# Moving stores and read-back loads from SyncE's DMA queue to GpSimd's in a fused attention and feed-forward kernel

## The chip, the cores and the metric

The kernel runs on one core of a Trainium2 chip. The metric is the device time of one execution in microseconds; shown is the median over the runs.

## The reference

```python
def _attn_ref(q, k, v, cap):                      # q, k, v: (4, 12, 448, 64) float32
    scale = 1.0 / np.sqrt(q.shape[-1])
    scores = scale * np.matmul(q, k.transpose(0, 1, 3, 2))
    scores = cap * np.tanh(scores / cap)          # cap = 30
    scores = scores - np.max(scores, axis=-1, keepdims=True)
    attn = np.exp(scores)
    attn = attn / (np.sum(attn, axis=-1, keepdims=True) + 1e-09)
    return np.matmul(attn, v).astype(np.float32)

def _moe_ref(x, w_in, w_out):                     # (1792, 768), (768, 2048), (2048, 768)
    h = x @ w_in
    g = h - np.tanh(h)
    return (g @ w_out).astype(np.float32)
```

x is the attention output with the heads of a token side by side. The two weights arrive as float64, everything else as float32.

## The kernel before

**Two streams of work.** Attention goes through 4 batches of 6 pairs of heads. Its scores are matmuls at `L735` (`fs`, from `fqst`, `fkst`, `fql`, `fkz`), emptied by ScalarE at `L743`; the exponentials are ScalarE's at `L828`, the values and row sums TensorE's at `L963` to `L987` and `L1054` to `L1062`, with sums over blocks of `fe` made by VectorE first (`fes`, `L922`, `L1029`, `L1037`). For some pairs the tails are folded: VectorE transposes and reduces (`fnum`, `fpart`, `L1089`, `L1092`) and TensorE multiplies `fpart` by a constant (`L1101`).

The feed-forward part goes through 64 steps of one slice of 128 hidden units each, for one batch at a time: `fh` = x times a slice of `w_in` (`L1425` to `L1427`, 18 matmuls of 128x384), ScalarE's tanh into `fg` (`L1438`), VectorE's `fg` = h - tanh h (`L1440`), a split of `fg` into a high part `fgh` and a low part `fgl`, and products with a slice of `w_out` that collect in the banks `facc` (`L1478`). The steps run as the segments (batch 0, slices 0 to 9), (1, 0 to 15), (0, 10 to 15), (2, all 16), (3, all 16). At the end of the first segment the sums of batch 0 are put into DRAM (`fyk`, `keep_y`, `L1641`) and read back when its other slices are due. Steps of the feed-forward part and pairs of the attention of later batches are interleaved.

**Weights.** A slice is used by up to four batches. The first time, its raw float64 words (`fw`) are loaded by SyncE's queue and decoded by VectorE in three passes (`L1278`, `L1285`, `L1292`) into `fu`, a tile of 128x1536 float32 (768 KB, the slice of `w_in` and that of `w_out` side by side). GpSimd's queue stores `fu` to DRAM as `fuk` (`L1220`, 16 stores). At the other 48 steps, 10 to 19 and 26 to 63, `fetch_w` loads it back (`fu<-fuk`, `L1209`) through SyncE's queue. There are two slots for `fu`. From `fu` each half is split: a cast to the high part `fwi` or `fwo` (`L475` where ScalarE does it, `L477` where VectorE does) and a subtraction for the low part on VectorE (`L486`). The same split makes `fkst`, `fqst`, `fgh` and `fxh`.

**Output.** A batch's sums are evicted to tiles `fo` and stored by `put` (`L1697`), through SyncE's queue except for one half of the very last one.

**What sets the order.** A planner in the kernel's own code (`Plan.schedule`) lays all instructions on five queues (TensorE, ScalarE, VectorE, SyncE, GpSimd) by a table of costs, with due times, the buffers' slots and the time at which each transfer lands, and the program is emitted in that order. An instruction that both ScalarE and VectorE can do (kind "AD", the casts) goes to VectorE only where ScalarE would be later by more than a bias; before 80 us of planned time the bias is the second number of a setting, later 500 ns. `run` plans with three settings (bias 0, 200, 500) and keeps the plan that ends first. A DMA's issue is priced in `dma`, 620 ns on SyncE and 600 elsewhere, and each queue may have seven transfers on the way:

```python
SETTINGS = [(0.0, 0.0), (0.0, 200.0), (0.0, 500.0)]
c = ISSUE + 60.0 * long if eng == "SP" else 600.0
```

Of the kernel before, what the change touches and what calls it, by code (L numbers as in the profile page):

```python
# [54 lines left out]

AHEAD = 3

BIAS, SWITCH = 500.0, 80000.0

EARLY_W = (10000.0, 40000.0)  # L60
# [20 lines left out]
LANES = 7  # L81

ISSUE, RAW_OUT = 620.0, "SP"
SLOW = dict(qk=2.3, v=2.1, w_in=2.0, w_out=0.95, kept=1.3, keep=0.75)


# [16 lines left out]
class Op:  # L103
    __slots__ = (
        "eng", "cost", "fn", "deps", "alloc", "later", "uses", "key", "due", "n", "succ", "need", "ready", "dma",
        "weight", "end", "lag", "glue",
    )


class Plan:  # L110
# [19 lines left out]
    def op(self, eng, cost, fn, deps=(), alloc=(), uses=(), key=1e18, dma=0.0, weight=1.0, lag=0.0):  # L130
        o = Op()
        o.eng, o.cost, o.fn, o.due, o.dma, o.weight, o.lag = eng, cost, fn, key, dma, weight, lag
        o.deps = [d for d in deps if d is not None]
        o.alloc, o.later = list(alloc), list(uses)
        o.uses = o.alloc + o.later
        o.glue = None
        o.n, o.succ = len(self.ops), []
        for d in o.deps:
            d.succ.append(o)
        for b in o.uses:  # L140
            b.users += 1
        self.ops.append(o)
        return o
# [6 lines left out]
    def schedule(self, wait, bias):  # L150
# [3 lines left out]
        for o in reversed(self.ops):  # L154
            o.key = o.due
            c = min(o.cost) if o.eng == "AD" else o.cost
            if o.dma:
                c += DMA_START + o.dma + DMA_END
            for s in o.succ:
                o.key = min(o.key, s.key - c - self.latency(o, s))  # L160
            o.need, o.ready, o.end = len(o.deps), 0.0, None
        for b in self.bufs:
            b.live, b.left, b.free_at, b.last, b.held = False, b.users, 0.0, None, 0.0
        engines = ["PE", "A", "D", "SP", "PL"]
        free = dict(zip(engines, START))
# [46 lines left out]
        def commit(t, e, o):  # L212

            nonlocal dma_free
            for b in o.alloc:
                s = slots[b.tag]
                b.slot = taken[b.tag] % len(s)
                s[b.slot] = None
                taken[b.tag] += 1
                b.live = True  # L220
            if e == "PE":
                free[e] = t + clock.run(t, o.cost, o.weight, True)
            else:
                free[e] = t + cost(o, e, t)
            o.end = free[e]
            if o.dma:
                begin = max(free[e] + DMA_START, dma_free)
                dma_free = begin + o.dma
                o.end = dma_free + DMA_END
                sent[e].append(o.end)  # L230
            order.append((o, e))
            if o in pools[e]:
                pools[e].remove(o)
            if o.eng == "AD":
                pools["D" if e == "A" else "A"].remove(o)
            for s in o.succ:
                s.ready = max(s.ready, o.end + o.lag + self.latency(o, s))
                s.need -= 1
                if not s.need:
                    put(s)  # L240
            for b in o.uses:
                b.left -= 1
                if b.bank and e != "PE":
                    b.last, b.held = e, o.end
                b.free_at = max(b.free_at, o.end + LAT)
                if not b.left:
                    slots[b.tag][b.slot] = b.free_at
            return 1

        for o in self.ops:  # L250
            if not o.need:
                put(o)
        left = len(self.ops)
        while left:
            cands = {}
            for e in engines:
                found = []
                for o in pools[e]:
                    t = start(o, e)
# [22 lines left out]
            t, e, o = best  # L282
            done = commit(t, e, o)
            while o.glue:
                o = o.glue
# [5 lines left out]
    def patient(self, e, cands, free, cost, wait):  # L291
# [17 lines left out]
                return c  # L309
        return None  # L310

    def run(self, settings, near=None, then=None, after=None):
        best = min((self.schedule(*s) for s in settings), key=lambda r: r[0])
        last = max(n for n, (o, e) in enumerate(best[1]) if e == "PE" or o is after)
        for n, (o, e) in enumerate(best[1]):
            if near and o.end > best[0] - NEAR:
                near()
                near = None
            for b in o.alloc:
                b.tile = self.make(b)  # L320
            if o.eng == "AD":
                o.fn(e)
            else:
                o.fn()
            if then and n == last:
                then()
# [33 lines left out]
class Build:  # L360
# [120 lines left out]
    def split(self, n, hi, lo, x, deps, allocs=((), ()), uses=((), ()), key=1e18, half=False):  # L481

        o1 = self.copy(n, hi, x, deps, allocs[0], uses[0], key=key, half=half)
        o2 = self.dve(
            n,
            lambda: self.nc.vector.tensor_sub(lo(), x(), hi().bitcast(F32)),  # L486
            [o1] + list(deps),
            allocs[1],
            uses[1],
            key=key,  # L490
        )
        return o1, o2

    def dma(self, eng, nbytes, fn, deps=(), alloc=(), uses=(), slow=1, long=False, key=1e18, lag=0.0):
        c = ISSUE + 60.0 * long if eng == "SP" else 600.0
# [44 lines left out]
    def fetch_qk(self, b, p, np_):  # L540
# [4 lines left out]
        for nm, src in (("q", self.q), ("k", self.k)):  # L545
            raw = self.plan.buf(nm + "raw", [128, 2, S // 32, 32])
            ops = []
            for i in range(4):
# [5 lines left out]
                def fn(i=i, h=h, dh=dh, raw=raw, src=src, queue=nc.scalar if eng == "A" else nc.sync):  # L554
# [6 lines left out]
                    self.dma(  # L561
                        eng, np_ * S * 128, fn, [], [] if ops else [raw], [raw] if ops else [], slow=SLOW["qk"],
                        lag=QK_LAG if (b, p) > (0, 1) else 0.0, key=-1e6 + 1e5 * p if also else 1e18,
# [5 lines left out]
    def fetch_v(self, b, p):  # L569
# [3 lines left out]
        for hp in range(2):  # L573
# [3 lines left out]
            for part in range(2):  # L577
# [4 lines left out]
                def fn(hp=hp, at=at, part=part, full=full, tail=tail, queue=nc.gpsimd if also else nc.sync):  # L582
# [3 lines left out]
                    else:  # L586
# [4 lines left out]
                        eng, (TAIL if part else FULL) * 256, fn, [], [] if ops else [vr],  # L591
                        [vr] if ops else [], slow=SLOW["v"], long=True, lag=V_LAG if (b, p) > (0, 0) else 0.0,
                        key=-5e5 + 1e5 * p if also else 1e18,
# [609 lines left out]
    def fetch_w(self, i, f):  # L1203

        nc, DM, plan = self.nc, self.DM, self.plan
        if f in self.kept_op:
            u = plan.buf("u", [128, 2, DM])
            o = self.dma(
                "SP", 8 * 128 * DM, lambda: nc.sync.dma_start(out=u(), in_=self.u_kept[f]), [self.kept_op[f]], [u],  # L1209
                slow=SLOW["kept"], lag=KEPT_LAG,  # L1210
            )
            return u, [o]
        raw, ops = self.fetch_raw(
            f, self.cast_ops[i - AHEAD][:1] if f >= self.segments[0][2] else [],
            key=EARLY_W[f] if f < len(EARLY_W) and not self.general else 1e18, lag=RAW_LAG,
        )
        u = plan.buf("u", [128, 2, DM])
        us = [self.decode(u, raw, ops)]
        o = self.dma(
            "PL", 8 * 128 * DM, lambda: nc.gpsimd.dma_start(out=self.u_kept[f], in_=u()), us, [], [u],  # L1220
            slow=SLOW["keep"], key=self.at + 40000,
        )
        self.kept_op[f] = o
        return u, us

    def fetch_raw(self, f, deps=(), key=1e18, lag=0.0):
# [4 lines left out]
        for hp in range(2):  # L1231

            def fn(hp=hp):
# [6 lines left out]
                self.dma(  # L1240
                    "SP", 4 * 128 * DM, fn, deps, [] if ops else [raw], [raw] if ops else [], slow=SLOW["w_in"], long=True, key=key,
                    lag=lag,
# [5 lines left out]
                RAW_OUT, 8 * 128 * DM, lambda: queue.dma_start(out=raw()[:, 1, :], in_=self.w_out[cols, :]),  # L1248
                deps, [], [raw], slow=SLOW["w_out"], key=key, lag=lag,
            )  # L1250
# [383 lines left out]
    def keep_y(self, m):  # L1634

        nc, k, self.y_ops[m] = self.nc, self.at + 3000, []
        for i in (0, 1, 2):
            o, ops = self.evict(i, self.plan.buf("o", [128, self.DM]), (), k)
            self.y_ops[m].append(
                self.dma(  # L1640
                    "SP", 512 * self.DM, lambda i=i, o=o: nc.sync.dma_start(out=self.y_kept[m][i], in_=o()), ops, [], [o],  # L1641
                    key=self.at + 20000,
                )
            )
        self.acc, self.acc_op = {}, {}
# [40 lines left out]
    def put(self, i, m, o, deps, cols):  # L1686
        nc, S, T = self.nc, self.S, self.TAIL
        if i < 3:
            r = S * m + 128 * i
            parts = [(slice(0, 128), self.out[r : r + 128, cols])]  # L1690
        else:

            tails = self.out.rearrange("(b s) c -> b s c", s=S)[2 * (i - 3) : 2 * (i - 3) + 2, self.FULL :, cols]
            parts = [(slice(T * j, T * j + T), tails[j]) for j in range(2)]
        for rows, out in parts:

            def fn(rows=rows, out=out, q=nc.scalar if cols.start else nc.sync):  # L1697
                q.dma_start(out=out, in_=o()[rows, cols])

            self.dma(  # L1700
                "A" if cols.start else "SP", (rows.stop - rows.start) * (cols.stop - cols.start) * 4, fn, deps, [],
                [o], key=self.at + 20000,
            )

# [129 lines left out]
```

## Time and profile before

| | us |
|---|---|
| median of 3 runs (lowest, highest) | 664.56 (664.21, 664.62) |
| the profiled execution, its whole time | 664.87 |
| its span in the trace | 663.1 |
| TensorE matmuls busy | 649.7 (98%) |
| VectorE busy | 505.3 (76%) |
| ScalarE busy | 444.5 (67%) |
| GpSimd busy | 24.9 (4%) |

The span runs from the first to the last instruction in the trace; the whole time has 1.8 us around it. The granted TensorE clock was 0.999 of full speed over the span. The chain of work that ended last is 85% TensorE, 6% VectorE, 4% ScalarE and 3% DMA. Issues of DMAs do not count as busy on SyncE.

### The profile page before, as it was taken

The page shows a single profiled execution, that of the slowest core. Times are in us where ns is not written, and L with a number is a line of the kernel's source. Part 1 is how long each engine was busy: PE and PEld are TensorE (multiplying, and loading weights), DVE is VectorE, ACT ScalarE, POOL GpSimd, SP SyncE. Part 2 cuts the span into 40 slices and gives each one's busy share as a digit, 9 for nine tenths or more (in the row PEclk, how much of TensorE's full clock was granted, in tenths as well). Part 3 has the DMA queues.
Part 4 walks back from the last instruction along what each step waited for, and adds up shares of the span by engine and source line. Part 5 has one row for each costly group of instructions (what it writes and reads, how often), then busy time and mean ns, then how long its engine had stood idle before and what let it go on. Part 6 is the DMA issues. An engine that isn't in the chain of part 4 may idle for free.

```text
span 663.1 us, 10078 instructions
## 1 busy us (share of the span) xinstructions
PE 649.7 (98%) x3690; PEld 535.6 (81%) x3690; DVE 505.3 (76%) x805; ACT 444.5 (67%) x760; POOL 24.9 (4%) x56
## 2 busy tenths in 40 slices
PE   8999999999999999999999999999999999999996
PEld 5333777786989898898797996987999999999996
DVE  5899999999997989999989599597573343433432
ACT  5999798875775474777874796795375545555444
POOL 5021000000000000000000000000000000000000
PEclk9999999999999999999999999999999999999999
DMA  9999999999793969768963967657776754456513
GB/s 136 201 208 229 307 202 266 242 236 237 234 211 122 245 205 259 229 217 268 255 190 111 276 191 211 199 144 210 235 265 188 191 142 139 133 158 191 148 43 124
DMA packets 156503, 132.59 MB, mean 200 GB/s; under 512 B 112544, under 2 KB 140896, under 8 KB 156448
## 3 DMA queue, kind: packets, MB, share of 16 engines
q1 hardware_dynamic: 149152, 115.89, 68.4%
q0 software_dynamic: 3424, 15.40, 6.6%
q10 hardware_dynamic: 3872, 0.59, 0.7%
q8 instruction: 31, 0.51, 0.3%
q14 instruction: 24, 0.20, 0.1%
HBM read 110.23 MB, written 21.63 MB: 199 GB/s over the span
## 4 chain that ended last, share of the span: by engine, by line
PE 85%; DVE 6%; ACT 4%; DMA 3%; issue 1%; SPq 0%; ACTq 0%; DVEq 0%
PE facc L1478 28%; PE fh L1425 11%; PE fh L1427 11%; PE fh L1426 11%; PE fs L735 6%; PE fs L972 5%; PE fs L1478 3%; PE fs L963 3%; PE fs L1054 2%; PE facc L764 2%; ACT fe L828 2%; DMA fw<-in_moe_w_out_dram 1%; ACT fe L743 1%; DMA fkraw<-in_k_dram 1%; PE fs L978 1%
## 5 line engine op out<-in xcount | busy, mean ns | idle before, releaser
L1478 PE MATMUL facc<-fwo,fgh 128*128 128x512 f32 (+1 forms) x768 | 166.2, 338 | 0.0
L1478 PEld LDWEIGHTS facc<-fwo,fgh 128*128 128x128 f32 x768 | 121.5, 188 | 17.3 <-issue 2.8
L1425 PE MATMUL fh<-fxh,fwi 128*128 128x384 f32 x384 | 131.6, 343 | 0.5 <-DVE fg L1440 0.5
L1427 PE MATMUL fh<-fxh,fwi 128*128 128x384 f32 x384 | 129.9, 338 | 0.0
L1426 PE MATMUL fh<-fxl,fwi 128*128 128x384 f32 x384 | 128.5, 335 | 0.0
L1478 PE MATMUL facc<-fwo,fgl 128*128 128x512 f32 (+1 forms) x384 | 98.8, 338 | 0.0
L828 ACT ACTIVATE fe<-fe,absc 128x896 f32<-128x896 f32 (+1 forms) x96 | 89.3, 962 | 1.3
L1440 DVE TENSOR_TENSOR fg<-fh,fg 128x384 f32<-128x384 f32 x64 | 35.4, 553 | 70.5 <-ACT fg L1438 70.3
L1425 PEld LDWEIGHTS fh<-fxh,fwi 128*128 128x128 f32 x384 | 72.1, 188 | 10.8 <-issue 4.9
L486 DVE TENSOR_TENSOR fwi<-fu,fwi 128x768 fp32r<-128x768 f32 x66 | 62.8, 952 | 19.5 <-ACT fwi L475 19.2
L1438 ACT ACTIVATE fg<-fh 128x384 f32<-128x384 f32 x64 | 31.2, 488 | 66.5 <-PE fh L1427 66.4
L1426 PEld LDWEIGHTS fh<-fxl,fwi 128*128 128x128 f32 x384 | 72.2, 188 | 0.5
L1427 PEld LDWEIGHTS fh<-fxh,fwi 128*128 128x128 f32 x384 | 72.0, 187 | 0.1
L475 ACT CAST fwi<-fu 128x768 fp32r<-128x768 f32 x53 | 44.2, 834 | 39.4 <-PE fh L1427 29.1
L743 ACT ACTIVATE fe<-fs 128x448 f32<-128x448 f32 x112 | 55.6, 542 | 15.7 <-PE fs L735 15.6
L486 DVE TENSOR_TENSOR fwo<-fu,fwo 128x768 fp32r<-128x768 f32 x66 | 62.6, 949 | 4.1 <-ACT fwo L475 3.9
L1478 PEld LDWEIGHTS facc<-fwo,fgl 128*128 128x128 f32 x384 | 58.7, 188 | 8.3
L475 ACT CAST fgh<-fg 128x384 fp32r<-128x384 f32 x54 | 27.7, 513 | 33.6 <-PE facc L1478 17.1
L735 PE MATMUL fs<-fqst,fkst 128*128 128x448 f32 x128 | 44.8, 370 | 2.0 <-ACT fqst L475 1.2
L972 PE MATMUL fs<-fe,fv 128*64 128x448 f32 x216 | 44.0, 542 | 0.0
L486 DVE TENSOR_TENSOR fgl<-fg,fgh 128x384 fp32r<-128x384 f32 x64 | 35.3, 551 | 9.2 <-ACT fgh L475 8.5
L735 PE MATMUL fs<-fql,fkz 128*128 128x448 f32 x112 | 41.0, 366 | 0.0
(205 smaller groups left out, 1038.4 us busy)
## 6 DMA issues: line engine op xcount, KB each, us to landing
fu<-fuk SPq DMA_DIRECT2D x48, 768.0 KB, 4.8
fw<-in_moe_w_in_dram SPq DMA_DIRECT2D x64, 384.0 KB, 6.4
fw<-in_moe_w_out_dram SPq DMA_DIRECT2D x32, 768.0 KB, 8.6
fuk<-fu POOLq DMA_DIRECT2D x16, 768.0 KB, 5.7
fqraw<-in_q_dram SPq DMA_DIRECT2D x44, 112.0 KB, 5.9
fkraw<-in_k_dram SPq DMA_DIRECT2D x44, 112.0 KB, 5.5
out_dram<-fo SPq DMA_DIRECT2D x12, 384.0 KB, 4.7
fv<-in_v_dram SPq DMA_DIRECT2D x44, 96.0 KB, 5.3
```

The costliest lines, as they stand in the source:

```text
L475: self.nc.scalar.copy(out(), in_())
L486: lambda: self.nc.vector.tensor_sub(lo(), x(), hi().bitcast(F32)),
L735: nc.tensor.matmul(ps()[:, :S], k, q, start=n == 0, stop=n == passes - 1)
L743: S, lambda: nc.scalar.activation(dst(), ps()[:, :S], AF.Tanh), [o],
L828: lambda: nc.scalar.activation(e()[:, :w, :], e()[:, :w, :], AF.Exp, scale=self.absc),
L972: nc.tensor.matmul(P()[D * h : D * h + D, :S], v1()[:, i, h, :], e()[:, h, :], start=i == 0, stop=False)
L1425: nc.tensor.matmul(h()[:, :n], wh, ah, start=(d == 0), stop=False)
L1426: nc.tensor.matmul(h()[:, :n], wh, al, start=False, stop=False)
L1427: nc.tensor.matmul(h()[:, :n], wl, ah, start=False, stop=(d == ND - 1))
L1438: n, lambda: nc.scalar.activation(g()[:, :n], h()[:, :n], AF.Tanh), [prev], [g], [h], psum=True, key=k
L1440: o = self.dve(n, lambda: nc.vector.tensor_sub(g()[:, :n], h()[:, :n], g()[:, :n]), [o], [], [g, h], key=k + 600)
L1478: nc.tensor.matmul(banks[bk]()[:, c0 : c0 + ne], lhs()[:, ts], w()[:, k, e0 : e0 + ne], start=bk in firsts and bk not in begun, stop=stop ...
```

## The change

The 48 loads of weights read back (`KEPT_Q`), the three stores of sums of batch 0 (`STORE_Q` in `keep_y`) and the nine output stores of batches 0 to 2 (`STORE_Q` in `put`, m < 3) are issued by GpSimd instead of SyncE, and the planner sees them on that queue. The last batch's output stores stay where they were, as do the loads of raw weights, of q, k and v, of the sums read back (`fo<-fyk`) and the 16 small loads of `fuk` for the last stretch. A pass that would hold loads back (`hold`) is added with a count of zero, so it does nothing.

```diff
+PASSES = 0
+HOLD = 30000.0
...
 ISSUE, RAW_OUT = 620.0, "SP"
+
+STORE_Q, KEPT_Q = "PL", "PL"
...
+    def hold(self):
+
+        for o in self.ops:
+            if o.eng == "SP" and o.dma and o.succ:
+                o.release = max(0.0, min(s.begin for s in o.succ) - HOLD)
+
     def run(self, settings, near=None, then=None, after=None):
+        for n in range(PASSES):
+            self.schedule(*settings[0])
+            self.hold()
...
+    def queue(self, eng):
+        return {"A": self.nc.scalar, "PL": self.nc.gpsimd, "SP": self.nc.sync}[eng]
+
...
             o = self.dma(
-                "SP", 8 * 128 * DM, lambda: nc.sync.dma_start(out=u(), in_=self.u_kept[f]), [self.kept_op[f]], [u],
+                KEPT_Q, 8 * 128 * DM, lambda: self.queue(KEPT_Q).dma_start(out=u(), in_=self.u_kept[f]), [self.kept_op[f]], [u],
                 slow=SLOW["kept"], lag=KEPT_LAG,
             )
...
-                    "SP", 512 * self.DM, lambda i=i, o=o: nc.sync.dma_start(out=self.y_kept[m][i], in_=o()), ops, [], [o],
+                    STORE_Q, 512 * self.DM, lambda i=i, o=o: self.queue(STORE_Q).dma_start(out=self.y_kept[m][i], in_=o()), ops, [], [o],
...
-            def fn(rows=rows, out=out, q=nc.scalar if cols.start else nc.sync):
-                q.dma_start(out=out, in_=o()[rows, cols])
+            eng = "A" if cols.start else STORE_Q if m < self.B - 1 else "SP"
+
+            def fn(rows=rows, out=out, eng=eng):
+                self.queue(eng).dma_start(out=out, in_=o()[rows, cols])
```

Lines of the kernel after stand 14 to 19 further down than the same lines before.

**The two queues, about 150 to 190 us.** SyncE before, from the last issues ahead of the first read-back (`fu` from `fuk_81`, for step 10):

```order
L555 DMA fkraw_1704<-in_k_dram 32x28x32
L585 DMA fv_111<-in_v_dram 128x3x64 x2
L587 DMA fv_111<-in_v_dram 64x64 x2
L1209 DMA fu_1751<-fuk_81 128x1536
L555 DMA fkraw_1704<-in_k_dram 32x28x32 x3
L1209 DMA fu_1847<-fuk_82 128x1536
L1209 DMA fu_1920<-fuk_83 128x1536
L1641 DMA fyk_0_130<-fo_1936 128x768
L1641 DMA fyk_1_131<-fo_1959 128x768
L1209 DMA fu_1985<-fuk_84 128x1536
```

GpSimd after, over the same work:

```order
L1237 DMA fuk_88<-fu_1492 128x1536
L1237 DMA fuk_89<-fu_1617 128x1536
L1226 DMA fu_1727<-fuk_81 128x1536
L1237 DMA fuk_90<-fu_1718 128x1536
L1226 DMA fu_1853<-fuk_82 128x1536
L1226 DMA fu_1921<-fuk_83 128x1536
L1658 DMA fyk_0_130<-fo_1936 128x768
L1658 DMA fyk_1_131<-fo_1966 128x768
L1226 DMA fu_1999<-fuk_84 128x1536
```

The read-backs leave the row of q, k and v loads and stand among the stores of kept tiles (`fuk<-fu`) and of sums.

**ScalarE at 66 to 72 us**, up to the last `fqst` cast, for which the score matmuls of `L735` wait (names are the scaled q, `fqst`, the keys, `fkst` and `fkz`, and step 0's `fg`). Before:

```order
L689 ACTIVATE fqst_815<-fqT_803,s_66 128x448
L808 ACTIVATE fe_819<-facc_182_779 128x448
L475 CAST fqst_815<-fqst_815 64x448 x2
L475 CAST fkst_97<-fkT_817 64x448
L475 CAST fkz_101<-fkT_817 64x448
L1438 ACTIVATE fg_848<-fh_808 128x384
L475 CAST fqst_815<-fqst_815 64x448
```

After:

```order
L706 ACTIVATE fqst_815<-fqT_803,s_66 128x448
L825 ACTIVATE fe_819<-facc_182_779 128x448
L489 CAST fqst_815<-fqst_815 64x448
L489 CAST fkst_97<-fkT_817 64x448
L489 CAST fqst_815<-fqst_815 64x448
L489 CAST fkst_97<-fkT_817 64x448
L1455 ACTIVATE fg_848<-fh_808 128x384
L489 CAST fkz_101<-fkT_817 64x448
L489 CAST fqst_815<-fqst_815 64x448
```

One `fkst` cast that VectorE did before is now on ScalarE, ahead of the last `fqst` cast. On VectorE the `fwi` subtraction of step 2 then moves behind a transpose of `fqT`, one of `fkT`, a `fwo` subtraction and an `fkst` subtraction that followed it before, or came later.

**VectorE at 444 to 450 us**, where the tail of one pair is folded (`fnum`, `fpart`) between the feed-forward steps. Before:

```order
L1114 RECIPROCAL fr_948_4694<-fs_4679 64x14 x2
L1089 STREAM_TRANSPOSE fnum_4697<-fes_4638 128x896
L1137 STREAM_TRANSPOSE frb_4706<-fr_948_4694 128x448
L1092 TENSOR_REDUCE fpart_4714<-fnum_4697 128x28
L1440 TENSOR_TENSOR fg_4692<-fh_4650,fg_4692 128x384
L486 TENSOR_TENSOR fwi_4683<-fu_4592,fwi_4683 128x768
```

After:

```order
L1131 RECIPROCAL fr_946_4683<-fs_4675 64x14 x2
L1054 TENSOR_TENSOR fes_4642<-fes_4642,fe_4574 64x448
L1154 STREAM_TRANSPOSE frb_4695<-fr_946_4683 128x448
L1106 STREAM_TRANSPOSE fnum_4697<-fes_4642 128x896
L1457 TENSOR_TENSOR fg_4699<-fh_4654,fg_4699 128x384
L1109 TENSOR_REDUCE fpart_4715<-fnum_4697 128x28
L500 TENSOR_TENSOR fwi_4693<-fu_4593,fwi_4693 128x768
```

The `fg` subtraction now stands ahead of the `fpart` reduction; on TensorE the matmul of `fpart` moves from just ahead of the next step's `fh` to behind six of its 18 matmuls.

Elsewhere between 68 and 450 us the order of VectorE and ScalarE differs in many small exchanges of this kind, and 6 casts in all move from VectorE to ScalarE. TensorE's order differs in some ten stretches; at 162 us it goes from the `facc` matmuls of step 7 straight to `fh` of step 9, where it ran eight score matmuls of `L735` between the two before. After 450 us the order of the three is the same.

## Rows read from the trace of the kernel before

**Rows 1.** The page's first part: busy us (share of the span) and instructions.

```profile
PE 649.7 (98%) x3690; PEld 535.6 (81%) x3690; DVE 505.3 (76%) x805; ACT 444.5 (67%) x760; POOL 24.9 (4%) x56
```

**Rows 2.** Stretches of 20 us: length, busy by engine, granted clock, DMA, GB/s.

```profile
60.00:80.00 20.00, 17.47 (x98) 12.50 (x95) 19.67 (x29) 16.23 (x29) 2.38 (x4) 1.00 1.05 263
...
460.00:480.00 20.00, 20.00 (x116) 18.83 (x115) 12.74 (x21) 8.60 (x14) 0.00 (x0) 1.00 0.87 253
```

**Rows 3.** Timeline of TensorE: start, us, work, [idle before <-what ended it].

```profile
62.53 0.97 PE L963 MATMUL fs<-fes,fones 128*64 128x448 f32 x4 [1.37 <-DVE fes L922]
...
71.94 0.67 PE L735 MATMUL fs<-fqst,fkst 128*128 128x448 f32 x2 [1.17 <-ACT fqst L475]
...
81.55 0.34 PE L1425 MATMUL fh<-fxh,fwi 128*128 128x384 f32 x1
...
162.33 0.58 PE L735 MATMUL fs<-fqst,fkst 128*128 128x448 f32 x2
...
164.32 0.47 PE L735 MATMUL fs<-fqst,fkst 128*128 128x448 f32 x1 [0.80 <-ACT fe L743]
...
303.56 0.34 PE L1425 MATMUL fh<-fxh,fwi 128*128 128x384 f32 x1
...
329.58 0.45 PE L1425 MATMUL fh<-fxh,fwi 128*128 128x384 f32 x1 [0.32 <-DVE fg L1440]
...
447.40 0.40 PE L1101 MATMUL fs<-fpart,fold 128*128 128x28 f32 x2 [0.64 <-DVE fpart L1092]
447.99 0.45 PE L1425 MATMUL fh<-fxh,fwi 128*128 128x384 f32 x1 [0.18 <-DVE fg L1440]
```

**Rows 4.** Waits of SyncE's queue: us in total, times, longest us.

```profile
SPq L1209 <- DVE fwo L486: 126.5, 29, 16.7
```

**Rows 5.** GpSimd's stores of kept tiles: duration ns min/median/max, first and last start us.

```profile
L1220 POOL DMA_DIRECT2D fuk<-fu x16: 532/532/762, 33.6 to 288.2; - x16
```

**Rows 6.** DMA issues: queue, count, size, median us from issue to landing.

```profile
fu<-fuk SPq DMA_DIRECT2D x48, 768.0 KB, 4.8
...
fuk<-fu POOLq DMA_DIRECT2D x16, 768.0 KB, 5.7
```

**Rows 7.** Timeline of SyncE's queue and ScalarE around step 10's read-back.

```profile
161.57 0.39 SPq L1209 DMA_DIRECT2D fu<-fuk  x1
...
167.10 0.83 ACT L475 CAST fwi<-fu 128x768 fp32r<-128x768 f32 x1
```

**Rows 8.** Timeline of GpSimd and VectorE at 128.5 us.

```profile
128.57 0.76 POOL L1220 DMA_DIRECT2D fuk<-fu  x1 [13.38 <-DVE fu L1292]
128.67 0.55 DVE L477 CAST fwi<-fu 128x768 fp32r<-128x768 f32 x1
```

**Rows 9.** Timeline of ScalarE, the cast that the score matmul waits for.

```profile
71.33 0.56 ACT L475 CAST fqst<-fqst 64x448 fp32r<-64x448 f32 x1
```

**Rows 10.** Timeline of VectorE, 68 to 82 us.

```profile
68.69 0.37 DVE L477 CAST fkst<-fkT 64x448 fp32r<-64x448 f32 x1
...
69.67 0.62 DVE L663 TENSOR_TENSOR fkst<-fkT,fkst 64x448 fp32r<-64x448 f32 x1
...
79.31 0.95 DVE L486 TENSOR_TENSOR fwi<-fu,fwi 128x768 fp32r<-128x768 f32 x1
80.18 0.64 DVE L615 STREAM_TRANSPOSE fqT<-fqraw 128x448 f32<-128x448 f32 x1
...
81.26 0.92 DVE L486 TENSOR_TENSOR fwo<-fu,fwo 128x768 fp32r<-128x768 f32 x1
```

**Rows 11.** Timeline of VectorE, 162 to 165 us.

```profile
162.46 1.09 DVE L922 TENSOR_TENSOR fes<-fe,fe 128x896 f32<-128x896 f32 x1
...
163.93 0.96 DVE L486 TENSOR_TENSOR fwi<-fu,fwi 128x768 fp32r<-128x768 f32 x1
```

**Rows 12.** Timeline of VectorE at 299.5 us, step 26's subtraction.

```profile
299.51 0.95 DVE L486 TENSOR_TENSOR fwi<-fu,fwi 128x768 fp32r<-128x768 f32 x1
```

**Rows 13.** Timeline of VectorE at 446 us, the reduction of the folded tail.

```profile
446.31 1.04 DVE L1092 TENSOR_REDUCE fpart<-fnum 128x28 f32<-128x896 f32 x1
```

More of the change, by code (lines that the diff above doesn't have):

```diff
@@ L105 @@
         "eng", "cost", "fn", "deps", "alloc", "later", "uses", "key", "due", "n", "succ", "need", "ready", "dma",
-        "weight", "end", "lag", "glue",
+        "weight", "end", "lag", "glue", "begin", "release",
     )
@@ L135, in op @@
         o.uses = o.alloc + o.later
-        o.glue = None
+        o.glue, o.release = None, 0.0
         o.n, o.succ = len(self.ops), []
@@ L160, in schedule @@
                 o.key = min(o.key, s.key - c - self.latency(o, s))
-            o.need, o.ready, o.end = len(o.deps), 0.0, None
+            o.need, o.ready, o.end = len(o.deps), o.release, None
         for b in self.bufs:
@@ L224, in commit @@
                 free[e] = t + cost(o, e, t)
-            o.end = free[e]
+            o.begin, o.end = t, free[e]
             if o.dma:
@@ L1695, in put @@
         for rows, out in parts:
-            def fn(rows=rows, out=out, q=nc.scalar if cols.start else nc.sync):
-                q.dma_start(out=out, in_=o()[rows, cols])
+            eng = "A" if cols.start else STORE_Q if m < self.B - 1 else "SP"
+            def fn(rows=rows, out=out, eng=eng):
+                self.queue(eng).dma_start(out=out, in_=o()[rows, cols])
             self.dma(
-                "A" if cols.start else "SP", (rows.stop - rows.start) * (cols.stop - cols.start) * 4, fn, deps, [],
+                eng, (rows.stop - rows.start) * (cols.stop - cols.start) * 4, fn, deps, [],
                 [o], key=self.at + 20000,
```

## The prediction

> **What bounds the kernel now.** I read the page's busy times first: TensorE is busy for 649.7 of 663.1 us [rows 1]. The table of 20 us stretches then shows where the rest is. A stretch in the second half holds 20.00 of 20 us of matmuls, while VectorE works 12.74 of 20; from 60 to 80 us TensorE holds only 17.47, with VectorE at 19.67 [rows 2]. The granted clock is 1.00 in both, the upper level (2.4 GHz), so the clock is no part of this case. What is left to gain is therefore a list of single stalls, and the timeline of TensorE names each with what ended it [rows 3]: 1.37 us at 62.53 (VectorE's `fes` sum), 1.17 at 71.94 (ScalarE's cast of `fqst`), 0.80 at 164.32 (ScalarE emptying a score bank), 0.32 at 329.58, and 0.64 and 0.18 at 447.40 and 447.99 (VectorE's `fpart` and `fg`). A last one, at 400 us, has its work in the same order after the change and is left out. The first loads and the work after the last matmul are not touched. None of these stalls ends with a DMA. So the transfers that the change moves are hidden now, and the ceiling of any gain is the sum of the idle times, 1.37 + 1.17 + 0.80 + 0.32 + 0.64 + 0.18 = 4.5 us, under 0.7%. A second thing to read is who waits for loads that are read back: SyncE stands for 126.5 us in front of them because VectorE's `fwo` subtraction has yet to free the slot [rows 4].
>
> **The change part by part.**
>
> The 48 read-backs (768 KB). An issue takes 0.53 us on GpSimd for this size [rows 5]: 60 moved issues (48 loads, 12 stores) put some 60 x 0.53 = 32 us on an engine that is nearly empty, nothing on TensorE. What matters is the landing: 4.8 us through SyncE; the nearest row for GpSimd is a store of the same size, 5.7 [rows 6]. I take 0 to 0.9 us later, nearer to 0.9. It is hidden where the slot comes free well before the tile's first cast. From landing to cast the 48 loads have from next to nothing, at the first of them, to over 8 us at the last, about 4 at the median. The first, for step 10, is tight: issued at 161.57, used by a cast at 167.10 [rows 7], 5.5 us for issue and landing. The one for step 36 is about as tight. For step 10 there is also a gain: its issue stood behind a run of q, k and v issues on SyncE, and on GpSimd only stores of kept tiles are ahead of it. Below nothing it may thus go by as much as it costs; I take 0. What is late next if that cover is gone is the cast of `fwi`, then its subtraction on VectorE, then the matmuls of `fh` (the second rival).
>
> GpSimd's queue. The loads now stand behind stores of kept tiles that wait for VectorE's decode. Only two loads are mixed with the last of the first ten stores, and a load of step 20 or later is issued long after the slot's user. The 12 output and kept stores wait for evictions, and a load behind one can be held by the little that the eviction is late; the loads of those steps have the 4 us above. I take 0. Nothing stands behind the loads that ends the kernel.
>
> A lock. At 128.57 a GpSimd issue took 0.76 us instead of 0.53 while VectorE ran a 128x768 cast at 128.67 [rows 5, 8]; in all three longest of the 16 such a cast ran, and the casts themselves were no longer. So a hit costs 0.23 us of landing: 3 of 16 of 48 loads is 9 hits, all hidden but for a tight load. The Trainium skill's page "SBUF — State Buffer" speaks against this change (section "SBUF: two separate sides", the box on the "DVE blocks DMA" trap): a GpSimd DMA cannot get its descriptors written while VectorE runs such a copy; the section on the bandwidth-pool intuition gives 620 ns alone against 3100 ns overlapped. By its figures a hit would cost 2.5 us (an estimate from that page), inside the 4 us of a typical load but not of a tight one, and one hit on a tight load would make the forecast 666.5. The rows agree that such a copy delays an issue, but by 0.23 us.
>
> SyncE relieved. Its other loads could go sooner, but nothing on TensorE waits for them: 0.
>
> The order of work. This is the larger part. The planner costs an issue on GpSimd otherwise than on SyncE and settles on another plan. From about 68 us on casts go from VectorE to ScalarE and both run in another order. Stall by stall, with the durations of before, where a move's bounds are the whole work moved and nothing:
> 1. 71.94: ScalarE casts one more 64x448 tile (the `fkst` that VectorE did at 68.69) ahead of the `fqst` cast of 71.33, which ends the stall. The `fqst` cast of the same shape takes 0.56 [rows 9]: +0.56.
> 2. 81.55: the `fh` matmul needs the `fwi` subtraction, which ended at 79.31 + 0.95 = 80.26, 1.29 early [rows 3, 10]. Now the transposes of `fqT` and `fkT`, the `fwo` subtraction and one `fkst` subtraction stand ahead of it, less the 0.37 of the cast gone. The first three ran from 80.18 to 82.18, so 2.00 + 0.62 - 0.37 = 2.25. TensorE arrives 0.56 later, so 2.25 - 1.29 - 0.56 = +0.40.
> 3. 164.32: TensorE now goes from the `facc` matmuls to `fh` of step 9 instead of the scores that waited. Its `fwi` subtraction ended at 163.93 + 0.96 = 164.89; a `fes` sum (1.09) and a 128x768 cast (0.55) ahead of it are now behind or elsewhere [rows 8, 11], others come ahead, some 2 us less in all. It is there by about 162.9. TensorE began those scores at 162.33 [rows 3] and comes 0.96 later by items 1 and 2, at 163.3, so it need not wait: -0.80, bounds -0.80 and 0.
> 4. 303.56: the subtraction of step 26 ended at 299.51 + 0.95 = 300.46, 3.1 early [rows 3, 12]. Two `fes` sums of the kind of 1.09, transposes and reciprocals now come ahead, about 4 us against 3.1 plus idle time that they fill: +0.3, bounds 0 and +1.0.
> 5. 329.58: `fg` of that step comes ahead of a sum that preceded it: -0.32.
> 6. 447.40 and 447.99: `fg` goes ahead of the `fpart` reduction that began at 446.31 and took 1.04 [rows 13], and TensorE runs six `fh` matmuls ahead of the one that needs `fpart`. `fg`, a pass over a 128x384 tile, then ends before 447, where TensorE is at 447.40 - 0.64 = 446.76: some 0.2 of the two stalls stays, so 0.2 - 0.64 - 0.18 = -0.62, bounds -0.82 and 0.
> The first matmul after a stall lasts 0.45 instead of 0.34 [rows 3]; three stalls go and two come: -0.11.
> Sum: 0.56 + 0.40 - 0.80 + 0.30 - 0.32 - 0.62 - 0.11 = -0.59 us. The profiled execution took 664.87 (span 663.1, 1.8 around it), 0.31 over the median of 664.56. So 664.28 for it, and 663.97, say 664.0, as a median.
>
> **The rivals.**
> R1, the moved work fills gaps and the new stalls (items 2 and 4) do not come, nor the 0.56, since VectorE's freed cast lets the rest move up: -0.80 - 0.32 - 0.62 and three first matmuls at 0.11, -2.07 in all, 662.5. For it: ScalarE, with 16.23 of 20 us from 60 to 80, has room. Against: VectorE, with 19.67, has none there [rows 2].
> R2, the other side: read-backs land late through GpSimd. Place: the two loads without slack, steps 10 and 36. Price: 0.9 of landing and 0.23 of lock each, 2.26; the 0.80 won at 164 just ahead of step 10's load would be lost in waiting for it. Then -0.59 + 0.80 + 2.26 = +2.47, 667.0. It outweighs the forecast's gain from 0.3 us of extra landing at each of the two, and is seen from about 0.7. For it: the 5.7 against 4.8 [rows 6]. Against: step 10's issue is freed of SyncE's other work.
> R3, the change does not do what it says: SyncE was in no one's way, and the new order wins as much as it loses, 664.6. For it: no stall ends with a DMA [rows 3], and the terms are of both signs.
>
> **How the numbers follow.** Forecast 0.42 (its own range 663.0 to 665.0), R1 0.25, R2 0.20, R3 0.13. Within 0.2% (1.33 us, about what a measurement of this kernel can tell from no change) is 663.2 to 665.9. Faster: 0.22 of R1 and 0.09 of the forecast, 0.31. Slower: 0.18 of R2 and 0.02 of the forecast, where the bounds of items 3 and 4 fall together, 0.20. Same: the rest, 0.49. The range takes in R1, down to where a part of the 1.17 us at 71.94 goes too, and the nearer half of R2: 661.9 to 666.8.
>
> **What would show it.** The profile after should show some 32 us of issues more on GpSimd, "fu<-fuk" with a landing of 4.8 to 5.7 us, and still no stall of TensorE that a load ends. The stall near 72 us should be about 1.7 us, a new one of 0.4 near 82 should stand before an `fh` matmul released by the `fwi` subtraction, those at 164 and 329 should be gone and those at 447 shrunk to some 0.2. Wrong would be a stall behind a `fwi` cast that waited for `fu` (R2), or new stalls of over a microsecond where the plan packs ScalarE anew, between 100 and 450 us.

## The result: 1.0% slower

The kernel after took 672.22 us (669.35 to 672.94 in three runs) against 664.56, a ratio of 1.0103 with a 95% interval of 1.0089 to 1.0117. Run again later beside the kernel before, it took 669.51 against 664.88, a ratio of 1.0080 (1.0058 to 1.0102). The forecast of 664.0 and its range of 661.9 to 666.8 were wrong, and the sign too.

**Where it sits.** The profiled execution after took 672.94, 8.07 more than that of before. Its page opens with the engines' busy times and the chain that ended last:

```profile
PE 652.0 (97%) x3690; PEld 536.4 (80%) x3690; DVE 503.1 (75%) x799; ACT 447.1 (67%) x766; POOL 57.6 (9%) x116
...
PE 78%; DVE 9%; DMA 6%; ACT 3%; issue 2%; SPq 0%; DVEq 0%; ACTq 0%; POOLq 0%
```

GpSimd has 57.6 us instead of 24.9, 32.7 more, near the 32 that the prediction's 60 issues at 0.53 made [rows 1, 5]. TensorE's work is the same, yet the span is 8.0 us longer, and DMA in the chain went from 3 to 6%. To find the place, look first at the copy that follows the last matmul. ScalarE's timeline has, before and after:

```profile
657.55 0.37 ACT L475 COPY fe<-fh 128x256 f32<-128x256 f32 x1 [3.29 <-PE fh L1578]
```

```profile
660.71 0.37 ACT L489 COPY fe<-fh 128x256 f32<-128x256 f32 x1 [3.29 <-PE fh L1595]
```

It comes 3.16 us later. The spans end at 663.1 and 671.1, so the stretch behind it grew from 5.5 to 10.4 us. **Five of the eight microseconds lie behind the last matmul**, where nothing of the change runs. The sequencers' rows there (line, queue, operation: shortest/median/longest ns, first and last start) tell what does. Before:

```profile
L1797 POOLq INC_SWDGE_SEM  x1: 927/927/927, 657.2 to 657.2; - x1
...
L1829 POOLq DRAIN  x3: 46/103/3086, 658.1 to 662.8; - x3
...
L1829 POOLq EVENT_SEMAPHORE  x4: 17/17/17, 662.3 to 663.0; - x4
```

After:

```profile
L1816 POOLq INC_SWDGE_SEM  x1: 2127/2127/2127, 660.1 to 660.1; - x1
...
L1848 POOLq DRAIN  x3: 46/109/7986, 662.2 to 670.8; - x3
L1848 SPq DRAIN  x3: 7/7/13, 664.6 to 670.5; - x3
```

At the end of the program every queue is drained, and the kernel ends when all are. GpSimd's drain took 3.09 us before, from 658.1 to 661.2, and all queues met at 662.3. After, it took 7.99, from 662.2 to 670.2. SyncE had finished its own part at 664.6 and stood until GpSimd came. The operation ahead of it on GpSimd, `INC_SWDGE_SEM`, went from 0.93 to 2.13.

**The other 3.2 us** lie in TensorE's order. Its timeline after (the rows from 64 us on that have a new or changed stall):

```profile
72.66 0.47 PE L752 MATMUL fs<-fqst,fkst 128*128 128x448 f32 x1 [1.76 <-ACT fqst L489]
...
84.42 0.44 PE L1444 MATMUL fh<-fxh,fwi 128*128 128x384 f32 x1 [0.24 <-DVE fwi L500]
...
127.68 0.47 PE L752 MATMUL fs<-fqst,fkst 128*128 128x448 f32 x1 [0.64 <-ACT fe L760]
...
212.60 0.45 PE L1442 MATMUL fh<-fxh,fwi 128*128 128x384 f32 x1 [0.18 <-DVE fg L1457]
...
293.61 0.47 PE L752 MATMUL fs<-fqst,fkst 128*128 128x448 f32 x1 [0.18 <-ACT fe L760]
...
355.38 0.44 PE L1442 MATMUL fh<-fxh,fwi 128*128 128x384 f32 x1 [0.18 <-DVE fg L1457]
...
468.57 0.44 PE L1442 MATMUL fh<-fxh,fwi 128*128 128x384 f32 x1 [0.18 <-DVE fg L1457]
...
488.23 0.44 PE L1442 MATMUL fh<-fxh,fwi 128*128 128x384 f32 x1 [0.57 <-DVE fg L1457]
```

Against [rows 3]: the stall at 72 us grew from 1.17 to 1.76, and those of 164, 329 and 447 us are gone; so is the one of 0.33 at 400 that the prediction left out as unchanged. There are new ones at 84 and 127, two of 0.18 at 293 and 355, and three (212, 468, 488) that were nowhere in the forecast's list. Behind the stall at 72 the table of stretches (length, busy by engine, granted clock, DMA, GB/s) has one thing more:

```profile
72.00:73.00 1.00, 0.34 (x2) 0.33 (x3) 1.00 (x2) 0.95 (x3) 0.00 (x0) 1.00 1.12 345
73.00:74.00 1.00, 1.00 (x7) 0.97 (x6) 1.00 (x2) 1.00 (x3) 0.00 (x0) 1.00 1.15 200
74.00:75.00 1.00, 1.00 (x5) 1.00 (x4) 1.00 (x3) 1.00 (x3) 0.00 (x0) 0.50 1.12 220
75.00:76.00 1.00, 1.00 (x4) 1.00 (x4) 1.00 (x1) 0.74 (x2) 0.00 (x0) 0.50 1.29 232
76.00:77.00 1.00, 1.00 (x4) 1.00 (x4) 1.00 (x2) 0.00 (x0) 0.00 (x0) 0.50 0.92 278
77.00:78.00 1.00, 1.00 (x6) 1.00 (x6) 0.36 (x1) 0.00 (x0) 0.00 (x0) 0.79 0.99 374
```

TensorE stood 1.76 us up to 72.66; from 74 us on the granted clock is 0.50, the lower level (1.2 GHz instead of 2.4), for some 3 us. Step 1's first matmul was 0.72 us later than before (0.12 of it older than the stall), step 2's, with no further stall between them, 2.13: the slower clock cost 1.4 us.

### The profile page after: what moved, and what is told of

It is laid out like the page before. It is cut to its first block, busy times and chain, and to the rows that moved or that the text cites. A ratio compares the mean times of both kernels' runs of the same rounds, so it can differ in the third digit from the quotient of the medians.

```text
span 671.1 us, 10122 instructions
## 1 busy us (share of the span) xinstructions
PE 652.0 (97%) x3690; PEld 536.4 (80%) x3690; DVE 503.1 (75%) x799; ACT 447.1 (67%) x766; POOL 57.6 (9%) x116
## 4 chain that ended last, share of the span: by engine, by line
PE 78%; DVE 9%; DMA 6%; ACT 3%; issue 2%; SPq 0%; DVEq 0%; ACTq 0%; POOLq 0%
PE facc L1495 24%; PE fh L1442 10%; PE fh L1444 10%; PE fh L1443 9%; PE fs L752 6%; PE fs L989 5%; PE fs L1495 3%; PE fs L980 3%; DMA fu<-fuk 3%; PE fs L1071 2%; PE facc L781 2%; DMA fqraw<-in_q_dram 1%; DVE fu L1302 1%; PE fs L995 1%; DVE fu L1309 1%
## 5 line engine op out<-in xcount | busy, mean ns | idle before, releaser
L1226 POOL DMA_DIRECT2D fu<-fuk x48 | 25.8, 538 | 337.3 <-DVE fwo L500 122.2
```

## The experiments

Theory after these readings: two costs of GpSimd's queue (its drain, and read-backs that land late) and one of the new order (the longer stall at 72 us with the clock behind it). Times stand beside those of the kernel before on the same chip.

**The order of after, issued by SyncE.**

```diff
-lambda: self.queue(KEPT_Q).dma_start(out=u(), in_=self.u_kept[f])
+lambda: nc.sync.dma_start(out=u(), in_=self.u_kept[f])
```

The planner still lays the loads and stores (the same edit is made there) on GpSimd's queue; only who issues them changes.

> The order of work of the kernel after, but the 48 read-backs and 12 stores are issued by SyncE again. Theory (two costs of GpSimd's queue, a longer last drain of about 4.9 us and read-backs that land late, 1.4 us; and the new order's stall at 72 us with a slower clock behind it, about 2): GpSimd's last drain is 3.1 us again, the read-backs land in some 4.9 us at the median, the stall at 72 us is still about 1.9 us with a granted clock below 1 behind it; time 666 to 667. Rival A (the new order itself makes the whole loss): 671 to 672. Rival B (the queue makes the whole loss): 664 to 665.

Measured 665.11 against 664.53, a ratio of 1.0012 (0.9994 to 1.0029). The whole loss of 5 to 8 us is gone with the queue, so the rival that blames the order falls. The time is also below the 666 to 667 expected, next to the rival in which the queue makes the whole loss. The drain is 3.09 again, and in this profile the clock behind the stall of 1.76 us at 72 is 1.00. But the ten runs go from 663.48 to 667.78. Every run has its mean granted clock on record: it is 0.996 in the three above 667, and 0.998 to 1.000 in six of the other seven (0.995 in the one of 664.92). What the order costs thus comes in some runs only.

**The order of before, issued by GpSimd.**

```diff
-lambda: nc.sync.dma_start(out=u(), in_=self.u_kept[f])
+lambda: nc.gpsimd.dma_start(out=u(), in_=self.u_kept[f])
```

The 12 stores are moved by the same edit in their two places.

> The order of work of the kernel before, with the 48 read-backs and 12 stores issued by GpSimd. Theory: GpSimd's last drain grows from 3.1 to about 8 us and stands alone behind the last matmul, +4.9; read-backs land late beside other loads, +1 to +2; the stalls at 72 and 164 us stay as before; time 670 to 671.5. Rival A (order): 664 to 665. Rival B (queue): 670 to 672, the same as the theory to the measurement; it is told from it by the run with the order of after on SyncE.

Measured 670.80 against 664.53, 1.0086 (1.0068 to 1.0103). The queue alone makes the loss. The drain is 7.99, the last copy starts at 659.40, 1.85 later than before, and that comes from two stalls:

```profile
346.64 0.44 PE L1425 MATMUL fh<-fxh,fwi 128*128 128x384 f32 x1 [1.13 <-DVE fg L1440]
...
352.77 0.38 PE L1101 MATMUL fs<-fpart,fold 128*128 128x28 f32 x2 [0.36 <-DVE fpart L1092]
```

**Sixty small DMAs more.** The kernel before, with 60 transfers of 256 bytes added on GpSimd's queue. They copy a constant to DRAM that nobody reads.

```diff
+        self.nc.sync.dma_start(out=u(), in_=self.u_kept[f])
+        for n in range(2 if self.loads % 4 == 0 else 1):
+            self.nc.gpsimd.dma_start(out=self.idle[self.loads][n : n + 1], in_=self.ones[0:1, 0])
```

> The kernel before, all its transfers where they were, and 60 DMAs of 256 bytes more on GpSimd's queue, one or two after each read-back. Theory that the last drain of GpSimd goes by the number of DMAs issued on its queue: drain about 8 us, time 669 to 670. Rival: it goes by the bytes or the descriptors that they moved: drain near 3.1 us, time within 0.5 us of the kernel before.

Measured 676.53 against 664.53. The drain row:

```profile
L1836 POOLq DRAIN  x3: 46/103/7990, 666.3 to 674.8; - x3
```

256 bytes or 768 KB make no difference to the drain: 97 DMAs give 7.99 us. The time missed the forecast by 7 us, though. The last copy starts 7.2 later than before, and nearly seven of them come between 304 and 320 us: TensorE waited 2.7 us for `fxl` loads of SyncE that were issued up to 7 us later than before, and behind the longest of these stalls, 2.1 us, the granted clock was 0.58 on average over 312 to 316 us. Many of the small DMAs had gathered behind the last stores of kept tiles just then. Why they held up SyncE's issues was not followed.

**Twelve instead of sixty.** The order of before, only the stores on GpSimd.

```diff
-lambda i=i, o=o: nc.sync.dma_start(out=self.y_kept[m][i], in_=o())
+lambda i=i, o=o: nc.gpsimd.dma_start(out=self.y_kept[m][i], in_=o())
...
-            def fn(rows=rows, out=out, q=nc.scalar if cols.start else nc.sync):
+            def fn(rows=rows, out=out, q=nc.scalar if cols.start else nc.gpsimd if m < self.B - 1 else nc.sync):
```

> The order of the kernel before, with only the 12 stores on GpSimd. Theory that the last drain grows by 0.082 us for each DMA on the queue (60 more took it from 3.09 to 7.99): 3.09 + 12 x 0.082 = 4.07 us, which sticks out by some 0.3 us; time 664.5 to 665. Rival (only the loads cost, for they bring data into SBUF): drain 3.1.

```profile
L1797 POOLq INC_SWDGE_SEM  x1: 1167/1167/1167, 658.3 to 658.3; - x1
...
L1829 POOLq DRAIN  x3: 46/109/4066, 659.5 to 664.2; - x3
```

4.07 us, as worked out beforehand: 37, 49 and 97 DMAs give 3.09, 4.07 and 7.99, which is 0.082 us for each; the operation ahead of it adds 0.020 for each (0.93, 1.17, 2.13). The one run took 666.31; of the 1.3 us or more that it lies over the forecast, 0.9 came before 64 us, ahead of anything that was changed.

**A drain where it is free.** The kernel after, with one more drain of GpSimd behind the last read-back.

```diff
+        self.queue(KEPT_Q).dma_start(out=u(), in_=self.u_kept[f])
+        if self.loads == 48:
+            self.nc.gpsimd.drain()
```

> The kernel after with one more drain on GpSimd, right behind the last of the 48 read-backs (about 611 us), where GpSimd has nothing else to do. Theory that the drain at the end goes through every DMA entry that GpSimd has left since the last drain: the early one takes some 8 us beside the matmuls, the last one falls well below 3 us, and the time falls by 4.5 to 5 against the kernel after, to 667 to 668. Rival (the last drain goes by the whole program's count, or waits for something else at the end): the last drain stays near 8 us and the time near 672.

Measured 665.24 against 664.53, 1.0005 (0.9994 to 1.0016). The two drains, the early one and the last, and the operation between them:

```profile
L1224 POOLq DRAIN  x1: 9250/9250/9250, 607.8 to 607.8; - x1
L1822 POOLq INC_SWDGE_SEM  x1: 181/181/181, 656.6 to 656.6; - x1
...
L1854 POOLq DRAIN  x3: 34/44/109, 656.8 to 661.7; - x3
```

The early one takes 9.25 us beside the matmuls, the last one at most 0.11. The early drain ends 4.0 us after the last read-back has landed, so it also waits for that landing. The last copy and the end of the span, at 661.9, leave 4.8 us for the stretch that took 10.4:

```profile
657.16 0.37 ACT L489 COPY fe<-fh 128x256 f32<-128x256 f32 x1 [3.29 <-PE fh L1601]
```

**One instruction takes back nearly the whole loss.** The time fell by more than the 4.5 to 5 us foreseen against the first runs of the kernel after, which had the slow clock or late loads too; against its second set it fell by 4.3. The ten runs part by their mean granted clock: six at 0.995 to 0.997 took 665.2 to 666.1, four at 0.998 to 1.000 took 663.6 to 664.8.

**The kernel after, again.**

> The kernel after, once more, beside the next three. By the last drain alone (4.9 us) and an order that costs nothing it would be 669.4; the first runs gave 669.4 to 672.9. If read-backs that land late and the slow stretch of the clock behind the stall at 72 us come and go, the runs spread from 669 to 673 and the profile shows either one, both or none of them; if they are fixed parts, all runs lie near 672.

Measured 669.51 against 664.88, four runs from 669.25 to 671.2. This profile has the 1.75 us stall at 72 us, with a clock of 1.00 behind it, and none of the stalls at 212, 468 and 488. Its last copy starts at 656.88, 0.67 *earlier* than before, and the 10.6 us behind it make the whole loss. So the drain is a fixed part, and the other 3 us of the first profile come and go. The seven runs of this kernel show it too: four with a mean granted clock of 0.994 to 0.996 took 669.3 to 669.5, three with 0.991 to 0.993 (two of them in the first set, and its median) took 671.2 to 672.9.

**The kernel before with an early drain.**

```diff
+        self.nc.gpsimd.dma_start(out=self.u_kept[f], in_=u())
+        if self.stores == 16:
+            self.nc.gpsimd.drain()
```

> The kernel before with one drain more on GpSimd, behind the last of its 16 stores of kept tiles (288 us). Theory: the last drain of 3.1 us goes; in the kernel before it was nearly hidden, ending about 1 us ahead of SyncE's part, but the stretch from the last matmul to the end of the span was 5.6 us there and 4.8 in the run with the early drain, so the time falls by 0.5 to 0.8 us, to 663.8 to 664.0. Rival: that part is hidden behind the landing of the last stores, no change, 664.5.

Measured 665.72 against 664.88, 1.0009 (0.9997 to 1.0021): no gain, the rival. The last drain is gone, but the stretch behind the last copy is 5.4 us as before (5.5). With 37 DMAs the drain is hidden behind ScalarE's last store, for whose landing (661.1 in the kernel before) SyncE waits at the end; with 97 it is not.

**What of the loss is landing.** The order of before on GpSimd, with the early drain (the 12 stores moved as well).

```diff
+        self.nc.gpsimd.dma_start(out=u(), in_=self.u_kept[f])
+        if self.loads == 48:
+            self.nc.gpsimd.drain()
```

> The order of the kernel before, read-backs and 12 stores on GpSimd, and the early drain. It leaves of GpSimd's queue only the later landing. Theory: matmuls end some 1 to 1.9 us later by read-backs that come late where their slack was under 1.5 us (steps 31, 32, 36), less 0.7 behind the last matmul: 664.8 to 665.7. Rival (late landing costs nothing): 663.8. Rival (most of the loss is landing): above 667.

Measured 666.24 against 665.21, 1.0026 (1.0007 to 1.0044): about 1 us stays (0.5 to 2.9 by the interval), half a microsecond above the range expected, and in its profile the last copy starts at 658.46, 0.91 later than before. The rows of the run on GpSimd without the early drain show how it comes about. SyncE's queue, GpSimd's, and VectorE:

```profile
329.97 2.31 SPq L1234 DMA_DIRECT2D fw<-in_moe_w_in_dram  x2
332.32 0.61 SPq L1248 DMA_DIRECT2D fw<-in_moe_w_out_dram  x1
...
334.86 0.53 POOL L1209 DMA_DIRECT2D fu<-fuk  x1 [9.65 <-DVE fwo L486]
...
343.69 0.56 DVE L477 CAST fwi<-fu 128x768 fp32r<-128x768 f32 x1 [4.87 <-DMA fu<-fuk]
```

The same transfers in the kernel before:

```profile
334.59 4.18 SPq L1209 DMA_DIRECT2D fu<-fuk  x2
338.82 1.30 SPq L1234 DMA_DIRECT2D fw<-in_moe_w_in_dram  x2
340.17 0.61 SPq L1248 DMA_DIRECT2D fw<-in_moe_w_out_dram  x1
```

Before, SyncE's queue took the transfers in their order: first two read-backs, each when its slot was free, then 1.5 MB of raw weights (`fw`, here for an inspection of the weights whose outcome is due at the end), whose last part landed at 349 without holding anything up. The read-back issued at 334.59 had the DMA engines nearly to itself and landed after 4.3 us. With the read-backs gone to GpSimd, SyncE has nothing to wait for; it issues the raw weights 8.9 us earlier, and the read-back issued at 334.86 shares the engines with them and lands after 8.7. VectorE stands 4.87 us for it, and TensorE the 1.13 at 346.64. With the early drain the same load took 7.7 and VectorE stood 3.8. The first profile of the kernel after has the same pair:

```profile
469.31 1.35 SPq L1251 DMA_DIRECT2D fw<-in_moe_w_in_dram  x2
470.70 0.85 SPq L1265 DMA_DIRECT2D fw<-in_moe_w_out_dram  x1
...
471.44 0.53 POOL L1226 DMA_DIRECT2D fu<-fuk  x1 [4.03 <-DVE fwo L500]
...
481.67 0.83 ACT L489 CAST fwi<-fu 128x768 fp32r<-128x768 f32 x1 [2.87 <-DMA fu<-fuk]
```

The load took 10.2 us, its cast waited 2.87 for it, and TensorE stood 0.57 at 488.23. In the second profile and in the one with the early drain the same load took 7.6 and 8.1, and no matmul waited. That the raw weights are what it shared with is read from the order of issues and landings; a run without those loads was not made.

**The stall at 72 us without GpSimd.** The kernel before, all on SyncE, planned with bias 500 alone:

```diff
-SETTINGS = [(0.0, 0.0), (0.0, 200.0), (0.0, 500.0)]
+SETTINGS = [(0.0, 500.0)]
```

> The kernel before, all transfers on SyncE as they were, planned with the third setting alone, which puts the second fkst cast on ScalarE as in the kernel after. Theory that this order alone brings the longer stall at 72 us (1.7 to 1.8 us of idle) and behind it, in some runs, a slower clock for some microseconds: most runs at 664 to 666 and one to three in ten above 667. Rival (the slower clock came with GpSimd's queue or by chance): no run more than 1.5 us above the median.

Measured 667.07 against 665.21, 1.0027 (1.0013 to 1.0042). Twelve runs fall into two lots, five from 665.1 to 665.8 and seven from 666.7 to 669.3. Its profile is one of the lower lot: a stall of 1.8 us at 72 and a clock of 1.00 behind it. A clock that falls explains only a part of the upper lot: three of its seven runs have a mean granted clock of 0.993 to 0.997 (669.29, 668.01, 666.71), which is within the one to three in ten expected, but the other four have 0.998 to 1.000 like the lower lot. What made those 2 us longer stays open; no profile of this kernel caught the upper lot.

**The kernel after with bias 0 and the early drain** (the drain as above).

```diff
-SETTINGS = [(0.0, 0.0), (0.0, 200.0), (0.0, 500.0)]
+SETTINGS = [(0.0, 0.0)]
```

> The kernel after with the early drain, planned with the first setting alone (bias 0), which leaves the order up to 72 us as in the kernel before. Theory that the added cast on ScalarE makes the stall there long enough for the clock to fall in some runs: stall 1.17 us of idle again, a clock of 1.00 behind it in every run, and time 663.5 to 664.5 with a narrow spread. Rival (the spread of the earlier run with the drain comes from the queue, not from the order): the spread of 663.6 to 666.1 stays.

Measured 664.27 against 664.88, 0.9993 (0.9983 to 1.0003), with the stall at 72 us back at 1.2 and the clock at 1.00. The spread, 663.26 to 665.88, hardly got narrower. The highest run is the only one with a mean clock below 0.998 (0.996); the other nine reach up to 664.70. A second, longer comparison:

> The kernel after with the early drain and the first setting alone, once more with more runs. Theory (matmuls end where they did before, and the stretch behind the last matmul is 0.7 us shorter): 663.9 to 664.3, 0.4 to 0.7 below the kernel before beside it. Rival (the 0.6 us of the first comparison are noise): within 0.2 us of it.

663.98 against 665.21, 0.9985 (0.9972 to 0.9998), with a mean clock of 0.998 or more in all twelve runs; two of them still took 665.6 and 666.2, so the clock is not all of the spread. This is the only version here below both kernels, by 0.6 to 1.2 us, which is at the edge of what can be told. Its matmuls end 0 to 0.4 us earlier than before, and the stretch behind them is 4.8 instead of 5.5.

**More room for the read-backs.** The same, with the planner told that they last 1.7 times as long:

```diff
-SLOW = dict(qk=2.3, v=2.1, w_in=2.0, w_out=0.95, kept=1.3, keep=0.75)
+SLOW = dict(qk=2.3, v=2.1, w_in=2.0, w_out=0.95, kept=2.2, keep=0.75)
```

> The kernel after with the early drain and the first setting, and the planner told that a read-back lasts 1.7 times as long (2.2 in place of 1.3 in its table), so that it lays them with more room. Theory that late read-backs cost some tenths: 663.5 to 664.0, with no cast that starts within 0.3 us of its read-back's landing. Rival (the order it finds stalls elsewhere): 664.5 or more.

Measured 682.51 against 665.21, 1.0260: a bad miss. The planner, believing the loads slow, lays everything else round them, and TensorE gets some twenty stalls of 0.1 to 1.4 us from 180 to 511 us, ended by ScalarE's and VectorE's work:

```profile
PE fs L752 <- ACT fe L760: 3.7, 7, 1.0
PE fh L1448 <- DVE fg L1463: 3.4, 4, 1.2
```

In this planner's table that one value could not be moved alone.

## Why the prediction was wrong, step by step

**The step that failed: "The first loads and the work after the last matmul are not touched", and "Nothing stands behind the loads that ends the kernel".** Both put the end of the program at 0. GpSimd's DMAs were priced at their issue, 0.53 us each on an idle engine, and at their landing. They have a third price, paid at the end of the program: 0.10 us each in GpSimd's last two operations (0.082 and 0.020), 6.1 us for 60. About 1.2 of that was still hidden behind the last store, and 4.9 stood alone. The place could have been read from the trace of before: the drain of 3.09 us was there, its end at 661.2 only 1.1 us ahead of the meeting of all queues at 662.3. That it grows with each DMA took the runs to show. The page's busy times leave such rows out, and the prediction read the page's GpSimd line, 24.9 us, as "nearly empty".

**The term for SyncE relieved, 0.** Wrong in sign. SyncE's waits, 126.5 us in front of read-backs [rows 4], were read as harmless. They also held back the raw weights queued behind, and so kept the DMA engines free for the read-back that was needed. This is the second rival's mechanism, and it cost about 1 us (1.0026) in the order of before where the drain was out of the way, but it has another cause and other places than were named. In the order of after with the early drain the time is level with before (1.0005), and its profile has no such stall. The landing through GpSimd was 5.6 us at the median in the first profile and 5.3 in the second, inside the 4.8 to 5.7 of the forecast:

```profile
fu<-fuk POOLq DMA_DIRECT2D x48, 768.0 KB, 5.6
```

What hurts is single loads of 8 to 11 us where they have no room; the kernel before had three such loads too, and no matmul waited for them. The load of step 10, named as the tight one, came off well: it was issued at 159.37 instead of 161.57 and landed over 3 us before its cast.

**The lock.** Of the 48 read-backs' issues after, the median is 0.530 us and the longest 0.836. Nine hits of 0.23 were foreseen; a cast of VectorE ran beside six of the 48, and it lengthened one:

```profile
L1226 POOL DMA_DIRECT2D fu<-fuk x48: 528/530/836, 159.4 to 611.4; - x48
...
215.91 0.84 POOL L1226 DMA_DIRECT2D fu<-fuk  x1 [4.43 <-DMA fu<-fuk]
...
216.07 0.56 DVE L491 CAST fwi<-fu 128x768 fp32r<-128x768 f32 x1 [0.45 <-PE fh L1444]
```

The issue ended at 216.75, 0.12 us after the cast. The page "SBUF — State Buffer" of the Trainium skill, section "A bandwidth-pool intuition that's wrong", has such a DMA blocked until VectorE's operation ends, and about 115 ns more; the trace agrees. No issue here took a third of the 3100 ns that the same section gives, from which the prediction made 2.5 us for a hit; the cast beside this one lasted 0.56.

**The order of work, -0.59.** The sum held, in part by luck. In the second profile of the kernel after the last copy comes 0.67 earlier than before, of which 0.29 was there by step 0, ahead of the change; with the early drain it is 0.39 earlier. The stalls from 66 us on add up to 0.47 less there than before, where items 1 to 6 make 0.48 less. But terms that were missed cancel: a new stall of 0.63 at 127 us stands against the 0.33 at 400 and some tenths in items 2 and 6. Item 1, +0.56: the stall went from 1.17 to 1.76, +0.59, and ScalarE's rows show the second `fkst` cast ahead. Item 2, +0.40: the matmul that needs the low part of `fwi` started 0.39 late (0.24 of it idle), and VectorE had itself stood 0.35 us for ScalarE's `fwi` cast, which the working did not have. Items 3 and 5: both stalls gone. Item 6: gone wholly, where 0.2 was to stay. Item 4, +0.3, came as some tenths of stalls at 293 and 355 us instead. Not foreseen: 0.64 at 127 us, ended by ScalarE, and the end of the stall at 400.

**The clock.** "The clock is no part of this case" was true of the profile of before. The longer stall of item 1 was followed in one profile by 1.4 us of lost time at the lower clock, and not in others with the same stall. Item 1 had a price for the stall alone.

**The rivals.** R2 had the right sign and was given 0.20, with a price of 2.47 against the 1 us measured for its mechanism. No rival had the drain, and the range, built from terms inside the span of the matmuls, could not reach it.

## What to carry to other kernels

Price a queue at three places: its issue, its landing, and what it leaves for the end of the program. For GpSimd here that was 0.1 us for each DMA, and a drain put where the engine is idle paid it for nothing. Before a wait on a queue is taken away, look at what is queued behind it: the order of one queue may be what keeps a needed transfer ahead of a large one that can wait. And a sum that ends at the last matmul is not yet a sum of the time.

## What the runs showed of the hardware that was not expected

- GpSimd's drain goes by the number of DMAs that its queue has had since the last drain, not by bytes: 3.09, 4.07 and 7.99 us for 37, 49 and 97, the same 7.99 for 256 bytes as for 768 KB. After an early drain the last one took 0.11 at most. An early drain of a queue with 97 DMAs ended 4.0 to 4.3 us after the last of them had landed (five profiles), with 37 DMAs 1.6 us after.
- The same order with the same stall of 1.75 us at 72 us ran on at a granted clock of 1.00 in one profile and at 0.50 for some 3 us in another. Over the runs without the long drain at the end that have a mean granted clock on record, it was 0.997 or less in 13 of 32 with an order that has this stall (after on SyncE, after with the early drain, before with bias 500), and in 5 of 117 with a stall of 1.17 there (the kernel before and the other versions). That the fall lies behind the stall was seen in one profile only.
- With the read-backs on GpSimd the stretch behind the last copy, without its drain, was 4.8 us; on SyncE it was 5.4. Up to 0.5 of these 0.6 us lies in ScalarE's last two issues, which took 1.20 us together with the early drain and 1.67 in the kernel before; why was not followed.
